# Another order of steps around the join behind attention and in the second experts' preparation

## The chip, the cores and the metric

The kernel runs on one core of a Trainium2 chip. The metric is the device time of one execution in microseconds. TensorE does matmuls, VectorE and ScalarE elementwise work and reductions, GpSimd (POOL) elementwise work and the indirect transfers; the SyncE queue (SP) issues the plain loads and stores.

## What is computed

Three layers, one behind the other, in float32: an attention with local and global keys, a mixture of experts with soft slots, and a mixture of experts in which each token takes its two best experts by noisy scores.

```python
def reference(**kwargs):
    attn_out = _attn_ref(**attn_kwargs)          # batch 2, 8 heads, 768 positions, head size 64
    x = np.ascontiguousarray(attn_out.transpose(0, 2, 1, 3)).reshape(B * S, H * D)   # 1536 x 512
    x = _moe_ref(x=x, **moe_kwargs)              # 32 slots in 8 experts, softmax over tokens and over slots
    return _moe2_ref(x=x, **moe2_kwargs)         # 8 experts, two per token

def _moe2_ref(x, w_gate, w_noise, noise, w1, w2):
    logits = x @ w_gate
    noise_scale = np.log1p(np.exp(x @ w_noise))
    noisy_logits = logits + noise_scale * noise
    top2 = np.argpartition(-noisy_logits, 2, axis=1)[:, :2]
    ...
            h = np.maximum(x[mask] @ w1[e], 0.0)
            out[mask] += top2_w[mask, k, None] * (h @ w2[e])
```

## The kernel before

**Attention** goes over 12 tiles of 128 tokens. While it runs, the soft slots' sums (maxima, exponentials, weighted tokens) are carried along by segments of tiles. **The join** (lines 541 to 612) adds the last tile: `psl` holds its logits in PSUM, `rn` the running negative maxima, `pm` gathers the maxima of the partition groups, `mneg` is their minimum. ScalarE copies the last tile's tokens from PSUM (`xl`, line 574), forms the factor of the old sums (`wun`, 581) and the new exponentials (`Et`, 582). TensorE adds up old sums (`joined`, 592) and the new tile (603) into `psi`, which VectorE copies to `siT` (608). `warm(k)` issues k matmuls whose result nobody uses. PE, DVE, ACT and POOL run in the order written here.

**The first experts** (`ffn_a`, `ffn_t`, `ffn_b`) start behind it: 8 experts, weights streamed in float32, the slots' 32 rows as stationary operand. Their result `op` in PSUM is copied in two halves into `os_` (770, 771), and eight matmuls (780) bring it into `soT`.

**The router** (954 to 991) forms the noisy scores: `ex` and `u_` are the exponential and one more than it, `ln` the logarithm (983), `t1` a correction of it (984 to 986). VectorE then takes the correction off, multiplies by the noise and adds the logits `pl` from PSUM (987 to 989) into `nl`, in which line 1005 looks for the best.

**The second experts** work in float16 pairs (high and low part). For each expert `e` a `Rank` object holds its steps, named by K0, K1, K2 for the first three: `w_abs(q)` (842) makes the maximum of a quarter of the second-layer weights on ScalarE, `w_scale_a` (850) joins the four on VectorE, `w_pow_a` (813) is a matmul that spreads it over the partitions, `w_pow_b` (821 to 828) makes the power of two by which the weights are scaled, `w_hi(q)` (871) writes a scaled quarter on ScalarE and `w_lo(q)` (874) the rest of it on VectorE; `inv` (922) keeps the inverse. `g_scale_a`, `g_hi`, `g_lo` and `g_put` do the same for the products of the first-layer weights with the slots' outputs (`Gst`). `pow_a` and `pow_b` do both powers of two in one.

The tokens are sorted into 24 slots of 128 rows, three per expert. `slot_h(j)` makes a slot's hidden values (1194), `slot_l` their low part (1203), and `slot_y(j)` is a generator of 24 matmuls (1282): for slots 0 and 1 each `next` issues two of them, and `go_on(ys, n)` calls `next` n times on each generator; for later slots each `next` issues eight. `add_out` adds the rows to the output by an indirect transfer (1300).

The order of slots 0 and 1 with the steps of K0, K1 and K2 is written out by hand from line 1487 on. For later slots the loop over `n` calls `do(n, place)` at the places "0", "l", "a", "m", "p", "e" and "b" between the blocks of eight matmuls, and `rank_steps` puts the steps of expert r at places counted in quarters of a slot from `BASE[r]`: `k(2, ...)` of expert 2 is place "m" of slot 3 and `k(3, ...)` its place "p".

Of the kernel before, what the change touches and what calls it, by code (L numbers as in the profile page):

```python
# [13 lines left out]
AF = mybir.ActivationFunctionType  # L14
ALU = mybir.AluOpType
# [46 lines left out]
def emit(tc, d, near=True, stop=None):  # L62
    nc = tc.nc
    es = ExitStack()
    with es:
# [122 lines left out]
        X = {}  # L188
# [361 lines left out]
        def warm(k):  # L550

            for _ in range(k):
                nc.tensor.matmul(pw, warmw[:, 0:128], warmw[:, 0:512], start=True, stop=True)
# [17 lines left out]
        if near:  # L571
            stX(NT - 1)
        xl = X["x", NT - 1]
        nc.scalar.activation(xl, X["pxx"].rearrange("p a q -> p (a q)"), AF.Copy)
        list(rest)
        mneg = cw.tile([128, 1], F32, name="mneg")
        nc.vector.tensor_reduce(mneg, pm, AX.X, ALU.min)
# [2 lines left out]
        wun = cw.tile([128, 1], F32, name="wun")  # L580
        nc.scalar.activation(wun, old, AF.Exp, bias=mneg, scale=-1.0)
        nc.scalar.activation(Et[P1], psl[P1], AF.Exp, bias=mneg[P1], accum_out=sg[P1])
        Wc = cw.tile([128, 32], F32, name="Wc")
        nc.vector.tensor_scalar(Wc, sel4[:, 0:32], wun, None, ALU.mult)
        sw = cw.tile([128, 1], F32, name="sw")
# [23 lines left out]
        nc.vector.tensor_scalar(rw, psum, 1e-9, None, ALU.add)  # L609
        nc.vector.reciprocal(rw, rw)  # L610
        nc.vector.tensor_copy(Ltok[:, NT - 1, :], pl_[:, 1, P1])
        warm(1)
        s_tail.close()
        s_ps.close()
        s_at.close()
# [31 lines left out]
        def pm_(shape, dt=F32):  # L647
            return ps_m.tile(shape, dt, name="m")
# [6 lines left out]
        def cut32(a, n):  # L655
            return more[:, a:a + n]

        wgn = cut32(0, 64).rearrange("p (c e) -> p c e", c=4)
        noise = cut32(64, 96).rearrange("p (t e) -> p t e", t=NT)
# [50 lines left out]
        def ring(i):  # L710
            return wst.tile([128, 2048], F32, name=f"w{i}")
# [10 lines left out]
        op = ps_y.tile([128, 512], F32, name="y")  # L722
# [45 lines left out]
        s_r.enter_context(tc.manual_schedule(engines=by_hand))  # L768
        os_ = wb.tile([128, 2048], F32, name=f"w{NWA + NW}")
        nc.scalar.activation(os_[:, 0:256], op[:, 0:256], AF.Copy)  # L770
        nc.scalar.activation(os_[:, 256:512], op[:, 256:512], AF.Copy)
        wy = ps_y.tile([128, 512], F32, name="y")

        def warm(k):
# [158 lines left out]
        K0, K1 = raw[0], raw[1]  # L933
# [22 lines left out]
        ttt = nc.vector.tensor_tensor  # L956
        gw = scratch([128, 4, 16], F32)
        ex, u_, ln, t1, rc, b_, nl = V("ex"), V("u_"), V("ln"), V("t1"), V("rc"), V("b_"), V("nl")
# [5 lines left out]
        pl = pm_([128, NT, 16])  # L964
# [19 lines left out]
        nc.vector.scalar_tensor_tensor(t1, u_, -1.0, ex, ALU.add, ALU.subtract)  # L984
        nc.vector.reciprocal(rc, u_)
        ttt(t1, t1, rc, ALU.mult)
        ttt(ln, ln, t1, ALU.subtract)
        ttt(ln, ln, noise, ALU.mult)
        ttt(nl, ln, pl[:, :, 0:8], ALU.add)
        K0.g_scale_a()  # L990
        nc.scalar.activation(gs0[:, 0:1], ex[:, 0, 0:1], AF.Exp)

# [193 lines left out]
        def slot_h(j, ct, hh=None, between=None):  # L1186
            e = j // OWN
            hh = wk3.tile([128, 2, 8, 128], F16, name="hh") if hh is None else hh
            phs = []
            for q in range(2):  # L1190
                ph = ps_h.tile([128, 4, 128], F32, name="h")
                for i in range(4):
                    f = 4 * q + i
                    nc.tensor.matmul(ph[:, i], Gst[:, e, 128 * f:128 * f + 128], ct, start=True, stop=True)  # L1194
                nc.scalar.activation(hh[:, 0, 4 * q:4 * q + 4], ph, AF.Relu)  # L1195
                phs.append(ph)
                if q == 0 and between:
                    between()
            return hh, phs
# [162 lines left out]
        def fetch(r, i):  # L1362

            t = xr(i) if i < 2 else ring(2 * ((r + 1) % 2) + i - 2)
            raw.setdefault(r, Rank(r, {})).u[i] = load_part(r, i, t)
# [3 lines left out]
        def at(j, place, f, *a):  # L1369
            steps.setdefault((j, place), []).append((f, a))  # L1370
# [5 lines left out]
        def rank_steps(r):  # L1376


            def k(place, nm, *a):
                j, q = divmod(BASE[r] + place, 4)  # L1380
                at(j, "0amp"[q], lambda: fetch(*a) if nm == "fetch" else getattr(raw[r], nm)(*a))

            first = r == 2
            if not first:
                k(-3, "g_mm")
            for i in range(2):
                if 2 < r < NE - 1:
                    k(-2, "fetch", r + 1, i)
            if not first:
                k(-2, "g_scale_a")  # L1390
                for q in range(4):
                    k((-4, -3, -1, 0)[q], "w_abs", q)
            if first:
                at(3, "l", K2.w_scale_a)
            else:
                k(0, "w_scale_a")
            k(2, "pow_a")
            k(2, "pow_b")
            k(3, "g_hi")
            k(4, "g_lo")  # L1400
            k(4, "w_hi", 0)
            k(4, "g_put", 0)
            k(5, "w_hi", 1)
            k(5, "g_put", 1)
            k(5, "w_lo", 0)
            k(6, "w_hi", 2)
            k(6, "w_lo", 1)
            if 2 < r < NE - 2:
                k(6, "fetch", r + 2, 2)
            k(8, "inv")  # L1410
            k(8, "w_hi", 3)
            k(9, "w_lo", 2)
            k(10, "w_lo", 3)
            if 2 < r < NE - 2:
                k(10, "fetch", r + 2, 3)
# [3 lines left out]
        for r in range(2, NE):  # L1419
            rank_steps(r)  # L1420
# [13 lines left out]
        def go_on(ys, n):  # L1434
            for _ in range(n):
                for y in ys:
                    next(y)
# [59 lines left out]
        for i in range(2):  # L1497
            K1.g_end(i, pst[i])
        h = slot_h(2, t)
        K1.w_pow_a()  # L1500
        K2.g_scale_a()
        go_on((y1,), 4)
        K1.w_pow_b()
        go_on((y0,), 2)
        list(y0)
        K1.w_hi(0)
        go_on((y1,), 4)
        list(y1)
        K1.w_hi(1)
        K0.inv()  # L1510
        K1.w_hi(1)
        K0.inv()
        h = slot_l(*h)
# [32 lines left out]
        with tc.If(over > 4):  # L1546
            t0, t1, t2, t3 = ring(0).bitcast(F16), ring(1), ring(2).bitcast(F16), ring(3).bitcast(F16)
# [205 lines left out]
```

## Time and profile before

| | us |
|---|---|
| median of 3 runs | 330.26 (330.18 to 330.68) |
| profiled execution, whole time | 330.27 |
| its span, first to last instruction | 328.2 |
| TensorE busy | 304.8 (93%) |
| ScalarE busy | 207.2 (63%) |
| VectorE busy | 200.1 (61%) |
| GpSimd busy | 132.4 (40%) |
| mean granted TensorE clock | 0.988 of full |

The busy shares are means over stages of different kinds, so the stages are read one by one below. In the rows, PE is TensorE, PEld its weight loads, DVE VectorE, ACT ScalarE; L and a number is a line of the kernel; times are microseconds from the span's start. What stands in brackets at a row's end is the idle time of the engine ahead of it and what ended that.

### The profile page before, as it was taken

The numbers are of one execution on the slowest core, as the hardware profiler recorded it, in microseconds if no ns is written. First come the engines' busy times: TensorE is split into PE (matmuls) and PEld (weight loads), VectorE is DVE, ScalarE is ACT, GpSimd is POOL, SyncE is SP. The second block draws the span as 40 slices with busy tenths as digits, with TensorE's granted clock in tenths as the row PEclk, the third lists the DMA queues.
The fourth block names the chain that finished last, engine by engine and source line by source line (L and its number), as shares of the span: only waits on it lengthen the run. The fifth ranks groups of instructions, "written<-read, shape, count | busy, mean of one in ns | idle before, by whom it ended". The sixth has DMA issues, their size and how long they took to land. (4 is left out here: it accounts for less than half of the span.)

```text
span 328.2 us, 7762 instructions
## 1 busy us (share of the span) xinstructions
PE 304.8 (93%) x2861; PEld 170.3 (52%) x2861; DVE 200.1 (61%) x723; ACT 207.2 (63%) x492; POOL 132.4 (40%) x165
## 2 busy tenths in 40 slices
PE   8699999999999999998989899999999999999990
PEld 3467776677775444344544444554454445544540
DVE  1965666656654100079787696978677595997210
ACT  2787777887632211089859795967778686785310
POOL 2364653554420010114450968561825445352131
PEclk9999999999997999999999999999999999999997
DMA  8999979847899999999899999489798943404342
GB/s 251 372 405 349 384 245 369 311 170 262 331 408 409 409 408 404 410 406 381 317 330 376 409 183 314 65 267 337 229 306 307 346 90 44 64 7 47 52 66 38
DMA packets 30571, 89.25 MB, mean 272 GB/s; under 512 B 2736, under 2 KB 6576, under 8 KB 30528
## 3 DMA queue, kind: packets, MB, share of 16 engines
q1 hardware_dynamic: 25840, 80.70, 65.1%
q0 software_dynamic: 4400, 7.48, 14.7%
q10 hardware_dynamic: 288, 0.52, 0.6%
q8 instruction: 24, 0.39, 0.5%
q14 instruction: 19, 0.16, 0.1%
HBM read 78.55 MB, written 10.14 MB: 270 GB/s over the span
## 5 line engine op out<-in xcount | busy, mean ns | idle before, releaser
L1282 PE MATMUL y<-w2hl,hh 128*128 128x512 f16 x552 | 125.0, 379 | 0.0
L1282 PEld LDWEIGHTS <-hh 128*128 128x128 f16 x552 | 52.2, 98 | 60.8 <-issue 3.5
L211 ACT ACTIVATE Tt<-Tt,nm 128x167 f32<-128x167 f32 x96 | 40.8, 428 | 20.7 <-DVE nm L204 20.6
L226 POOL TENSOR_TENSOR Pb<-Tt,r 128x668 f32<-128x668 f32 x24 | 31.6, 1318 | 47.8 <-DVE r L218 26.5
L1203 DVE SCALAR_TENSOR_TENSOR hh<-h,hh 128x512 f16<-128x512 f32 x46 | 29.5, 683 | 20.3 <-ACT hh L1195 20.2
L1300 POOL DMA_INDIRECT out_y<-ys,sidx x15 | 28.0, 1863 | 28.5 <-ACT ys L1294 14.4
L874 DVE SCALAR_TENSOR_TENSOR w2hl<-w,pm,w2hl 128x1024 f16<-128x1024 f32 x28 | 35.2, 1279 | 4.1 <-ACT w2hl L871 3.2
L1318 POOL DMA_INDIRECT cT<-ctab,gidx x25 | 29.5, 1179 | 12.0 <-issue 6.8
L204 DVE CUSTOM_DVE_ANT_0 Tt<-s,bias 128x167 f32<-128x167 f32 x96 | 26.0, 327 | 11.8 <-PE s L200 10.1
L1195 ACT ACTIVATE hh<-h 128x512 f16<-128x512 f32 x46 | 25.1, 595 | 12.1 <-PE h L1194 11.9
L871 ACT ACTIVATE w2hl<-w,pm 128x1024 f16<-128x1024 f32 x29 | 32.4, 1146 | 0.2 <-DVE pm L827 0.2
L842 ACT ACTIVATE w2hl<-w 128x1024 f16<-128x1024 f32 x28 | 29.5, 1056 | 0.0
L236 PE MATMUL pt<-c,Pb 128*128 128x128 f32 x176 | 26.5, 282 | 2.9 <-ACT PT L240 1.6
L240 ACT ACTIVATE PT<-pt 128x512 f32<-128x512 f32 (+1 forms) x48 | 26.0, 546 | 2.3 <-PE pt L236 2.3
L200 PE MATMUL s<-kx,qd 64*64 64x167 f32 x384 | 22.4, 313 | 4.1 <-DVE nm L204 3.0
L1300 POOL DMA_INDIRECT out_y<-c,sidx x7 | 12.5, 1789 | 32.0 <-DVE hh L1203 14.9
L236 PEld LDWEIGHTS pt<-c,Pb 128*128 128x128 f32 x176 | 18.6, 141 | 11.3 <-ACT PT L240 4.1
L259 PE MATMUL px<-PT,vt 128*64 128x128 f32 x352 | 22.3, 277 | 0.2
L200 PEld LDWEIGHTS s<-kx,qd 64*64 64x64 f32 x384 | 14.9, 132 | 11.0 <-PE pt L236 5.0
L259 PEld LDWEIGHTS px<-PT,vt 128*64 128x64 f32 x352 | 18.9, 137 | 3.0 <-issue 1.9
L211 ACT ACTIVATION_READ_ACCUMULATOR Tt<-Tt,nm 128x1 f32 x96 | 18.5, 193 | 0.0
L704 PE MATMUL h<-w,siT 128*32 128x256 f32 x256 | 16.4, 404 | 0.0
(314 smaller groups left out, 445.5 us busy)
## 6 DMA issues: line engine op xcount, KB each, us to landing
w<-in_w2b SPq DMA_DIRECT2D x14, 1024.0 KB, 7.4
x<-in_w1b SPq DMA_DIRECT2D x12, 1024.0 KB, 14.4
w<-in_w1a SPq DMA_DIRECT2D x16, 512.0 KB, 7.7
w<-in_w2a SPq DMA_DIRECT2D x16, 512.0 KB, 6.6
w<-in_w1a SPq DMA_DIRECT2D x8, 1024.0 KB, 8.6
w<-in_w2a SPq DMA_DIRECT2D x8, 1024.0 KB
vt<-in_va SPq DMA_DIRECT2D x6, 512.0 KB, 8.0
out_y<-w2hl SPq DMA_DIRECT2D x1, 3072.0 KB
```

What stands on the lines that cost most here:

```text
L200: nc.tensor.matmul(st[t][r:r + 64, n % 2, :], qd[T % NQ][g, p, 64 * t:64 * t + 64], kx[g, p, a:a + 167], start=True, stop=True, tile_posit ...
L211: nc.scalar.activation(Tt[:, k], Tt[:, k], AF.Exp, bias=nm[:, k:k + 1], scale=-1.0, accum_out=st[:, k:k + 1])
L226: nc.gpsimd.tensor_tensor(wide(Pn, 33, 264 + 64, 528, 167), Pu.rearrange("p (a t) c -> p a t c", t=2), rb(167), ALU.mult)
L236: nc.tensor.transpose(pt[:, ch, t], Pn[:, 2 * (n % 2) + t, 136 * ch:136 * ch + 128], ident)
L259: nc.tensor.matmul(px[64 * h:64 * h + 64, p, :], vv[:, c:c + 64], cols_, start=(ch == 0 or m == 0), stop=(ch == 1))
L842: nc.scalar.activation(w2hl[:, self.r, 1, 2 * q:2 * q + 2], self.quarter(q), AF.Abs, accum_out=self.wm[:, q:q + 1])
L871: nc.scalar.activation(w2hl[:, self.r, 0, 2 * q:2 * q + 2], self.quarter(q), AF.Copy, scale=self.sw)
L874: nc.vector.scalar_tensor_tensor(w2hl[:, self.r, 1, 2 * q:2 * q + 2], self.quarter(q), self.sw, w2hl[:, self.r, 0, 2 * q:2 * q + 2], ALU.m ...
L1203: nc.vector.scalar_tensor_tensor(hh[:, 1, 4 * q:4 * q + 4], phs[q], 0.0, hh[:, 0, 4 * q:4 * q + 4], ALU.max, ALU.subtract)
L1282: nc.tensor.matmul(py, hh[:, hx, f], w2hl[:, e, wx, f], start=(n == 0), stop=(n == 23))
L1300: o = nc.gpsimd.indirect_dma_start(out=out, out_offset=bass.IndirectOffsetOnAxis(ap=sidx[:, j:j + 1], axis=0), in_=ys, in_offset=None, com ...
L1318: nc.gpsimd.indirect_dma_start(out=cgf[:, place(n)], out_offset=None, in_=ctab, in_offset=bass.IndirectOffsetOnAxis(ap=gidx[:, n:n + 1], a ...
```

## The change

Seven small moves, with no new function:

- In the join, ScalarE's copy into `xl` stands behind the two exponentials instead of ahead of them, and one `warm(1)` at its end goes.
- The second half of the copy into `os_` goes from ScalarE to VectorE.
- The router's sum is formed as (logits - correction x noise) + logarithm x noise instead of (logarithm - correction) x noise + logits.
- `pow_a` and `pow_b` of expert 2 move from place "m" of slot 3 to its place "p", ahead of `g_hi`.
- `K1.w_pow_a` moves behind `K2.g_scale_a` and behind eight matmuls of slot 1.
- `K1.w_hi(1)` and `K0.inv()`, which stand there twice, are made once.

```diff
         xl = X["x", NT - 1]
-        nc.scalar.activation(xl, X["pxx"].rearrange("p a q -> p (a q)"), AF.Copy)
         list(rest)
...
         nc.scalar.activation(Et[P1], psl[P1], AF.Exp, bias=mneg[P1], accum_out=sg[P1])
+        nc.scalar.activation(xl, X["pxx"].rearrange("p a q -> p (a q)"), AF.Copy)
...
         nc.vector.tensor_copy(Ltok[:, NT - 1, :], pl_[:, 1, P1])
-        warm(1)
...
         nc.scalar.activation(os_[:, 0:256], op[:, 0:256], AF.Copy)
-        nc.scalar.activation(os_[:, 256:512], op[:, 256:512], AF.Copy)
+        nc.vector.tensor_copy(os_[:, 256:512], op[:, 256:512])
...
         ttt(t1, t1, rc, ALU.mult)
-        ttt(ln, ln, t1, ALU.subtract)
+        ttt(t1, t1, noise, ALU.mult)
+        ttt(t1, pl[:, :, 0:8], t1, ALU.subtract)
         ttt(ln, ln, noise, ALU.mult)
-        ttt(nl, ln, pl[:, :, 0:8], ALU.add)
+        ttt(nl, ln, t1, ALU.add)
...
-            k(2, "pow_a")
-            k(2, "pow_b")
+            k(2 + first, "pow_a")
+            k(2 + first, "pow_b")
             k(3, "g_hi")
...
         h = slot_h(2, t)
-        K1.w_pow_a()
         K2.g_scale_a()
         go_on((y1,), 4)
+        K1.w_pow_a()
         K1.w_pow_b()
         go_on((y0,), 2)
         list(y0)
         K1.w_hi(0)
         go_on((y1,), 4)
         list(y1)
-        K1.w_hi(1)
-        K0.inv()
         K1.w_hi(1)
         K0.inv()
```

## Rows read from the trace of the kernel before

**Rows 1.** Table of stretches: us; busy us per engine, instructions in brackets; clock, DMA share, GB/s.

```profile
180.00:200.00 20.00, 19.02 (x133) 9.47 (x132) 16.19 (x39) 16.70 (x31) 15.53 (x14) 1.00 0.98 312
200.00:220.00 20.00, 20.00 (x140) 10.20 (x138) 16.90 (x52) 15.72 (x27) 12.22 (x14) 1.00 0.73 183
```

**Rows 2.** Timeline of the join: start us, us, engine, line, operation, out and in.

```profile
98.50 0.27 DVE L578 COPY Lsb<-psl 32x128 f32<-32x128 f32 x1
98.63 0.60 ACT L574 ACTIVATE xs<-pt 128x512 f32<-128x512 f32 x1 [2.63 <-PE pt L276]
...
99.12 0.28 ACT L581 ACTIVATE wun<-rn,mneg 128x1 f32<-128x1 f32 x1
99.31 0.34 ACT L582 ACTIVATE Et<-psl,mneg 32x128 f32<-32x128 f32 x1
...
100.94 1.06 PE L603 MATMUL o<-Et,xs 128*128 128x32 f32 x8
...
102.37 0.61 PE L553 MATMUL pt<-c 128*128 128x512 f16 x1
...
102.50 0.17 DVE L611 COPY Ltok<-s 128x32 f32<-128x32 f32 x1
...
102.91 4.92 PE L704 MATMUL h<-w,siT 128*32 128x256 f32 x64
```

**Rows 3.** Stretches of half a microsecond, TensorE alone: busy us, granted clock, DMA share, GB/s.

```profile
102.00:102.50 0.50, 0.50 (x4) 0.59 1.05 418
...
105.50:106.00 0.50, 0.50 (x16) 0.99 1.06 426
```

**Rows 4.** Timeline, the copies of the slot outputs.

```profile
136.64 0.38 ACT L770 ACTIVATE w<-y 128x256 f32<-128x256 f32 x1 [5.63 <-PE y L750]
...
137.08 1.08 PE L780 MATMUL m<-c,w 128*128 128x32 f32 x8 [0.50 <-ACT w L770]
```

**Rows 5.** Timeline, the last slot's copy, split between VectorE and ScalarE.

```profile
319.76 0.48 DVE L1291 TENSOR_SCALAR ys<-y,gsc 128x256 f32<-128x256 f32 x1 [6.87 <-PE y L1282]
320.29 0.47 ACT L1292 ACTIVATE ys<-y,gsc 128x256 f32<-128x256 f32 x1 [5.01 <-DVE ys L1291]
```

**Rows 6.** Timeline, the router: first operation behind the logarithm, and the search.

```profile
142.35 0.26 DVE L987 TENSOR_TENSOR w2hl<-w2hl 128x96 f32<-128x96 f32 x1 [0.16 <-ACT w2hl L983]
...
143.29 0.92 DVE L1005 MAX8 w2hl<-w2hl 128x8 f32<-128x8 f32 x12
```

**Rows 7.** Timeline of TensorE at expert 1's power of two.

```profile
166.68 0.61 PE L1194 MATMUL h<-ct,Gst 128*128 128x128 f16 x8
...
168.92 0.23 PE L813 MATMUL m<-identb,wx 128*128 128x128 bf16 x1 [1.63 <-DVE wx L850]
...
168.98 1.89 PE L1282 MATMUL y<-w2hl,hh 128*128 128x512 f16 x8
...
170.71 1.03 PE L1282 MATMUL y<-w2hl 128*128 128x512 f16 x4
```

**Rows 8.** Timeline, ScalarE's scaled quarters of expert 1.

```profile
173.99 3.36 ACT L871 ACTIVATE w2hl<-w,pm 128x1024 f16<-128x1024 f32 x3
```

**Rows 9.** Loads issued in 141 to 142.5 us (last: landing), and the timeline's first use.

```profile
w<-in_w2b SPq DMA_DIRECT2D x2, 1024.0 KB, 8.0
...
158.83 1.06 ACT L842 ACTIVATE w2hl<-w 128x1024 f16<-128x1024 f32 x1
```

**Rows 10.** Timeline at expert 2's powers of two, and its scaled rows.

```profile
183.13 0.22 PE L813 MATMUL m<-identb,gm 128*128 128x128 bf16 x1
...
184.11 0.16 DVE L850 TENSOR_REDUCE wx<-wm 128x1 f32<-128x4 f32 x1 [1.98 <-ACT w2hl L842]
...
184.40 3.62 PE L1282 MATMUL y<-w2hl,hh 128*128 128x512 f16 x16
...
191.80 0.73 DVE L919 COPY Gst<-Gst 32x1024 f16<-32x1024 f16 x1
...
193.53 0.61 PE L1194 MATMUL h<-ct,Gst 128*128 128x128 f16 x8
```

## The prediction

> **What bounds the kernel now.** I read the table of stretches first [rows 1]. In 200 to 220 us TensorE is busy all the time at the full clock, and the three stretches after it, up to 280 us, read the same; in 180 to 200 it lacks 0.98 us. From about 184 us on the end is therefore TensorE's start plus a fixed row of matmuls: what lets that row start one microsecond earlier ends the kernel one microsecond earlier. Before that point the chain runs through several engines, so I went along the timeline and looked at the places that the diff touches: the join behind attention at 98 us, the copies at 137 us, the router's VectorE chain at 142 us, and the second experts' preparation at 166 to 194 us. The question in each is which wait ends last.
>
> The transfers are the other candidate: the DMA share is 0.98 in 180 to 200 us [rows 1]. But no compute instruction of the path waits for a load after 92 us. The second-layer weights of expert 1, issued from 141.3 on, land 8.0 us later, by about 150, and ScalarE first reads them at 158.83 [rows 9]: about 9 us in hand, more than all that I forecast.
>
> **The join: copy moved behind the exponentials.** The join's row of work is ScalarE's copy (98.63), its exponential of the old maxima (99.12), its exponential of the new logits (99.31), then VectorE and TensorE. The exponentials stand behind the copy only by ScalarE's order: the copy takes the slot from 98.63 to 99.12, 0.49 us [rows 2]. What the first exponential needs VectorE writes just ahead of its own copy at 98.50; the second reads the PSUM tile that this copy reads from 98.50 to 98.77, and in the new order it starts at about 98.82, just behind. So everything from here to the first expert's matmul moves by 0.49 us. The moved copy would end at about 99.8; its readers, the join's last eight matmuls (100.94 before), would start at 100.45, so other work covers it by 0.6 us. Were it later than that, only the amount beyond would count.
>
> **The join: one warm-up matmul removed.** It starts at 102.37 and takes 0.61 us, and the first expert's matmul starts at 102.91, although VectorE's last copy, for which it waits, ended at 102.67 [rows 2]. Handing over from VectorE costs about 0.05 us where a row shows it [rows 5], so the start could have been 102.72: 0.18 us lost. With both edits the experts start 0.67 us earlier, at about 102.23.
>
> **What the clock takes back.** The granted clock falls to its lower level, 1.2 GHz, at 102.1 us, behind a join in which TensorE has only small matmuls, and is at 2.4 GHz again from 105.5 (0.50 in all six half-microseconds between the two rows) [rows 3]. If that low stretch stays where it is, the 0.67 us of earlier start are worked at half speed: by 105.5 the kernel before has done (105.5 - 102.9)/2 = 1.30 us of full-speed work, the changed one (105.5 - 102.23)/2 = 1.63. The gain is 0.33 us; if the low stretch moves along with the work it is 0.67. I take 0.33, since nothing ahead of 98.6 moves, and keep both ends.
>
> **The split copy of the slot outputs.** The second half goes from ScalarE to VectorE. TensorE starts on the first half at 137.08, and its eight matmuls stand evenly (0.28 us each, 1.08 in all, so one per 0.114) [rows 4]: none of them waited for the second half, and the fifth, the first that needs it, is due at 137.54. A faster second half wins nothing. It could lose: at the end of the kernel one PSUM tile is split in the same way, and there ScalarE starts at 320.29, when VectorE's 0.48 us are over, after an idle wait for it [rows 5]. One behind the other, VectorE would end at 136.64 + 0.38 + 0.48 = 137.50 plus 0.05 or 0.1 of handing over. Price: 0 (side by side) to 0.1 us; I take 0, as 137.5 is still about when it is due.
> The Trainium skill (PSUM — Partial Sum Buffer, "PSUM bank collisions raise a hardware error") says that ScalarE and VectorE must not read the same partitions of one bank at once, so that software has to put them in sequence; the trace agrees, with 320.29 behind 319.76 + 0.48. By that rule this part of the sum is a loss of 0 to 0.1 us, by the opposite it is 0.
>
> **The router's chain.** Before, three VectorE operations follow the logarithm, and the first waited 0.16 us for ScalarE until 142.35; the search starts at 143.29, so they take 0.94, or 0.31 each [rows 6]. After, two operations run ahead without the logarithm and two follow: four from about 142.2. In a strict chain that is 4 x 0.31 = 1.25, ending at 143.44, a loss of 0.15; with the third overlapped, since it does not depend on the two ahead of it, the loss is about 0. I take 0.05 us. It is on the path: the search follows at once.
>
> **Expert 1's power of two, placed later.** TensorE ends the hidden matmuls that start at 166.68 (eight of them, some 0.05 us apart) by about 167.1 and then stands until 168.92 (1.63 us idle by the profile), because the little matmul next in its queue needs a maximum that VectorE gives only then. Behind it stand eight matmuls of slot 1, from 168.98 to 170.71, which need nothing of it [rows 7]. The change puts these eight ahead. They take 1.73 us, run from about 167.1 to 168.85, and the little matmul still starts at about 168.92. What followed at 170.71 then starts at 168.97: 1.74 us gained. VectorE's reading of the result is not delayed, and ScalarE's copy of slot 0 and the scaled quarters behind it move along.
>
> **Steps made twice removed.** One of ScalarE's three scalings that start at 173.99 and take 3.36 us is the second copy of the same step: about 1.1 us of ScalarE [rows 8], and a tiny VectorE operation. TensorE waits for neither directly. Their worth is that all later ScalarE work of this stretch, among it expert 2's absolute maxima, comes 1.1 us earlier on top of the 1.74.
>
> **Expert 2's power of two, one place later.** TensorE's next stall is of the same kind: one little matmul at 183.13, the other only behind VectorE's last maximum of expert 2 (184.11, it had waited 1.98 us for ScalarE), and slot 3's last eight matmuls not before 184.40 [rows 10]. The change puts both little matmuls behind those eight. With the 1.74 and 1.1 us above, the maximum is there at about 181.3, while the pair is due at about 183.1, so it does not stall again. Gained: 184.40 - 183.13 = 1.27 less the pair's own 0.12 (0.06 each, from 168.92 to 168.98 in [rows 7]) = 1.15 us. In exchange the chain behind the pair stands later in the order: the scaled rows of expert 2, copied last by VectorE from 191.80 to 192.53 and first used by TensorE at 193.53, 1.00 us in hand [rows 10]. TensorE moves by 1.74 + 1.15 = 2.89. If this chain moves by as much, nothing is lost; if only by the 1.74, it costs 2.89 - 1.74 - 1.00 = 0.15. I take 0. No transfer is moved past another; the loads issued behind these steps go out earlier with them.
>
> **The sum.** 0.33 - 0 - 0.05 + 1.74 + 1.15 = 3.17 us. The profiled execution took 330.27 us (span 328.2 and 2.07 around it) and the median is 330.26, so no scaling is needed: 330.27 - 3.17 = 327.1 us.
>
> **Rivals.**
> The clock stays up. The new join is denser, shorter by 0.67 us. If the clock then does not fall, the start gains its 0.67 and the 1.30 us lost at half clock besides: 1.97 in place of 0.33, giving 325.5 us. For it: the fall came only at the very end of the join [rows 3]. Against it: up to 102.1 the new order holds nearly the same matmuls. Chance 0.16. The Trainium skill (TensorE: Matmul & The Clock Gate, "The HAM clock gate") says that TensorE's activity sets its clock and that the moment of a change varies from run to run; the fall at 102.1 agrees with the first, no row here shows the second.
> The gain is partly given back at expert 2's first slot. If its scaled rows do not move at all, TensorE waits 2.89 - 1.00 = 1.89 us there (329.0); halfway between that and the 0.15 above it is 328.1 us. For it: VectorE is busy 16.2 of 20 us there [rows 1], and the pair stands 1.73 us later in TensorE's order. Against it: ScalarE's queue gets 1.1 us free. Chance 0.14.
> The transfers set the pace after all. If the weights of experts 3 and 4 had no slack, TensorE would wait for them in 180 to 200 us and end where it does now, 330.2 us. For it the DMA share of 0.98 [rows 1], against it the 9 us of [rows 9]. Chance 0.05.
> Slower: the clock stays down. Without the warm-up matmul the low stretch could be longer. At half clock each microsecond of dense work costs 0.5; to eat 3.17 us the clock would have to stay down 6.3 us beyond 105.5, to about 112 us, and from there on the kernel is slower: with 114 us it takes 331.4. Against it: the experts' matmuls follow without a gap, and they brought the clock back at 105.5 before [rows 2, 3]. Chance 0.04.
>
> **How the numbers follow.** The forecast has 0.61, with its own range 326.5 to 327.7 (the bounds 0.33 to 0.67 at the join, 0 to 0.25 lost at copy and router, 0.15 at expert 2). For 8 in 10 the range reaches to the free clock, 325.3, and into the partly lost gain, 328.4. A difference of 0.2%, 0.66 us, is about what a measurement of this kernel tells from none. Faster by more: the forecast, the free clock and the partial loss, 0.91; within: the transfers, 0.05; slower: 0.04.
>
> **What would show it.** In the new profile the first expert's matmul starts near 102.2; TensorE has no idle wait for a maximum near 167 to 169 and none near 181 to 183; slot 3's last eight matmuls start some 3 us earlier; the busy row of 200 to 280 us stays unbroken and ends earlier by the same. I am wrong if a wait of TensorE appears ahead of expert 2's first slot near 190 us, if a load is what an engine waits for, or if the low clock lasts beyond 106 us.

## The result and the profile after

The changed kernel takes 328.38 us (median of 11 runs, 327.45 to 329.87) beside 331.48 us for the kernel before, measured with it (11 runs, 329.4 to 334.39): a ratio of 0.9907 with a 95% interval of 0.9879 to 0.9935. The forecast of 327.1 us was 0.9904 of the 330.26 us known then. The profiled execution after took 327.62 us, with a span of 325.7; before it was 330.27 and 328.2. Both kernels scatter by 2 to 5 us from one execution to the next; a section below shows one cause. Executions more than 1.5% above the fastest of their kernel are left out of all ratios, so a ratio need not be that of two medians.

The rows after are shown in the order of the rows before; line numbers are those of the kernel that ran, so they differ by one here and there. First the table of stretches (us; busy us of PE, PEld, DVE, ACT, POOL; clock, DMA share, GB/s), which answers to [rows 1]:

```profile
180.00:200.00 20.00, 20.00 (x141) 10.03 (x139) 14.28 (x35) 16.06 (x30) 13.40 (x15) 1.00 1.01 332
200.00:220.00 20.00, 20.00 (x141) 10.29 (x140) 16.69 (x52) 14.57 (x25) 13.62 (x15) 1.00 0.76 179
```

The 0.98 us that TensorE lacked in 180 to 200 us are filled. The join, against [rows 2]:

```profile
98.38 0.27 DVE L577 COPY Lsb<-psl 32x128 f32<-32x128 f32 x1
98.49 0.29 ACT L580 ACTIVATE wun<-rn,mneg 128x1 f32<-128x1 f32 x1 [2.62 <-DVE mneg L576]
98.76 0.36 ACT L581 ACTIVATE Et<-psl,mneg 32x128 f32<-32x128 f32 x1
...
99.12 0.57 ACT L582 ACTIVATE xs<-pt 128x512 f32<-128x512 f32 x1
...
100.32 1.06 PE L603 MATMUL o<-Et,xs 128*128 128x32 f32 x8
...
101.88 0.17 DVE L611 COPY Ltok<-s 128x32 f32<-128x32 f32 x1
...
102.11 1.08 PE L703 MATMUL h<-w,siT 128*32 128x256 f32 x8 [0.36 <-DVE Ltok L611]
```

Counted from VectorE's copy into Lsb, the first exponential comes 0.51 us sooner (0.11 us behind it, before 0.62), the join's last eight matmuls 0.50 sooner (1.94, before 2.44), and the first expert's matmul 0.68 sooner (3.73, before 4.41). The moved copy ends at 99.69, 0.63 us ahead of its readers at 100.32. The first expert's matmul now starts 0.06 us behind the end of the copy it waits for.

The copies of the slot outputs and the router, against [rows 4] and [rows 6]:

```profile
136.09 0.38 ACT L769 ACTIVATE w<-y 128x256 f32<-128x256 f32 x1 [5.63 <-PE y L749]
136.51 0.42 DVE L770 COPY w<-y 128x256 f32<-128x256 f32 x1 [3.76 <-ACT w L769]
136.53 1.09 PE L779 MATMUL m<-c,w 128*128 128x32 f32 x8 [0.50 <-ACT w L769]
...
141.26 0.26 DVE L985 TENSOR_TENSOR w2hl<-w2hl 128x96 f32<-128x96 f32 x1
...
142.66 0.92 DVE L1005 MAX8 w2hl<-w2hl 128x8 f32<-128x8 f32 x12
```

VectorE starts behind ScalarE's copy (136.09 + 0.38 = 136.47), so the halves go one after the other, as at the kernel's end [rows 5], and TensorE's eight matmuls take 1.09 us in place of 1.08.

ScalarE's scaled quarters of expert 1, two in place of the three of [rows 8]:

```profile
172.40 2.18 ACT L870 ACTIVATE w2hl<-w,pm 128x1024 f16<-128x1024 f32 x2
```

TensorE at expert 1's power of two, and then at expert 2's, against [rows 7] and [rows 10]:

```profile
166.80 0.61 PE L1194 MATMUL h<-ct,Gst 128*128 128x128 f16 x8 [0.60 <-ACT ct L1101]
167.24 1.89 PE L1282 MATMUL y<-w2hl,hh 128*128 128x512 f16 x8
168.97 0.22 PE L812 MATMUL m<-identb,wx 128*128 128x128 bf16 x1
169.03 1.03 PE L1282 MATMUL y<-w2hl 128*128 128x512 f16 x4
...
173.85 0.33 PE L1194 MATMUL h<-ct,Gst 128*128 128x128 f16 x3 [0.29 <-DVE ct L1103]
...
180.03 3.62 PE L1282 MATMUL y<-w2hl,hh 128*128 128x512 f16 x16
183.49 0.22 PE L812 MATMUL m<-identb,gm 128*128 128x128 bf16 x1
183.54 0.22 PE L812 MATMUL m<-identb,wx 128*128 128x128 bf16 x1
183.60 1.89 PE L1282 MATMUL y<-w2hl,hh 128*128 128x512 f16 x8
185.33 0.61 PE L1194 MATMUL h<-ct,Gst 128*128 128x128 f16 x8
```

Both waits for a maximum are gone: the eight matmuls of slot 1 stand where TensorE stood still, and the pair of expert 2 runs through behind sixteen matmuls. Two new waits, 0.60 and 0.29 us, are taken up below. From slot 2's hidden matmuls (L1194) to the last slot's copy the kernel before takes 319.76 - 166.68 = 153.08 us [rows 5, 7], the changed one 317.25 - 166.80 = 150.45. This stretch is the measure used below, since it shuts out most of what happens ahead of it; where the part ahead ends some 2 us early (e4, e5, e7 below) even this stretch changes by some 0.3 us.

### The profile page after: what moved, and what is told of

It reads as the page before. It is cut to its first block, busy times and chain, and to the rows that moved or that the text cites. A ratio compares the mean times of both kernels' runs of the same rounds, so it can differ in the third digit from the quotient of the medians.

```text
span 325.7 us, 7762 instructions
## 1 busy us (share of the span) xinstructions
PE 304.1 (93%) x2860; PEld 170.2 (52%) x2860; DVE 199.6 (61%) x724; ACT 206.0 (63%) x490; POOL 131.8 (40%) x165
## 5 line engine op out<-in xcount | busy, mean ns | idle before, releaser
L1300 POOL DMA_INDIRECT out_y<-ys,sidx x15 | 27.0, 1797 | 27.4 <-ACT ys L1294 14.2
L1318 POOL DMA_INDIRECT cT<-ctab,gidx x25 | 28.5, 1141 | 12.0 <-DVE w2hl L1203 5.5
L870 ACT ACTIVATE w2hl<-w,pm 128x1024 f16<-128x1024 f32 x28 | 31.2, 1147 | 0.2 <-DVE pm L826 0.2
L1300 POOL DMA_INDIRECT out_y<-c,sidx x7 | 13.9, 1982 | 33.9 <-DVE hh L1203 14.9
L211 ACT ACTIVATION_READ_ACCUMULATOR Tt<-Tt,nm 128x1 f32 x96 | 18.5, 193 | 0.0
```

The source lines that it names most:

```text
L211: nc.scalar.activation(Tt[:, k], Tt[:, k], AF.Exp, bias=nm[:, k:k + 1], scale=-1.0, accum_out=st[:, k:k + 1])
L870: nc.scalar.activation(w2hl[:, self.r, 0, 2 * q:2 * q + 2], self.quarter(q), AF.Copy, scale=self.sw)
L1300: o = nc.gpsimd.indirect_dma_start(out=out, out_offset=bass.IndirectOffsetOnAxis(ap=sidx[:, j:j + 1], axis=0), in_=ys, in_offset=None, com ...
L1318: nc.gpsimd.indirect_dma_start(out=cgf[:, place(n)], out_offset=None, in_=ctab, in_offset=bass.IndirectOffsetOnAxis(ap=gidx[:, n:n + 1], a ...
```

## The experiments

"Tail" is that stretch, "join" goes from VectorE's maximum of the last tile's logits (L565) to the first expert's matmul (before 6.04 us, after 5.36). Ratios are times over those of the kernel before, measured with each run, with 95% intervals.

**Each of the three edits of the second experts alone.** On the kernel before, the power of two of expert 1 placed later:

```diff
-        K1.w_pow_a()
         K2.g_scale_a()
         go_on((y1,), 4)
+        K1.w_pow_a()
         K1.w_pow_b()
```

> The kernel before with one move alone: expert 1's little power-of-two matmul behind the eight matmuls of slot 1. My theory (TensorE's two stalls are the bulk): the idle 1.63 us ahead of that matmul goes, everything behind is 1.74 us earlier, the stall at expert 2's powers stays (about 1.0 to 1.3 us, since ScalarE's queue is still as long); time 1.7 us less. Rival (the gain is at the join and in ScalarE's load, the stall is refilled by the next wait): 0 to 0.4 us less.

Ratio 0.9946 (0.9927 to 0.9966); tail 151.37 us, 1.71 less. TensorE in the timeline:

```profile
169.73 0.23 PE L813 MATMUL m<-identb,wx 128*128 128x128 bf16 x1
...
183.42 0.23 PE L813 MATMUL m<-identb,wx 128*128 128x128 bf16 x1 [0.98 <-DVE wx L850]
```

The first stall goes and the second stays, whole. Stall 1 is worth what the prediction gave it (1.74).

On the kernel before, expert 2's pair one place later:

```diff
-            k(2, "pow_a")
-            k(2, "pow_b")
+            k(2 + first, "pow_a")
+            k(2 + first, "pow_b")
```

> The kernel before with expert 2's two little matmuls one place later, alone. My theory: slot 3's last eight matmuls run at once, the wait for VectorE's maximum at 183 to 184 us disappears behind them, 1.15 us less, and the first stall (1.63 us at 167 to 169) stays. Rival (the wait returns at the first use of expert 2's scaled rows, which had 1.0 us in hand): a wait of TensorE ahead of that use near 193 us and less than half of the gain, 0 to 0.5 us.

Ratio 0.9959 (0.9931 to 0.9988); tail 152.16, 0.92 less. The pair no longer waits, and up to slot 5's hidden matmuls 1.15 us are won (20.02 us behind slot 2's, before 21.17); but then expert 2's first slot waits for its scaled rows:

```profile
192.96 0.74 DVE L919 COPY Gst<-Gst 32x1024 f16<-32x1024 f16 x1
193.75 0.45 PEld L1194 LDWEIGHTS <-Gst 128*128 128x128 f16 x8 [0.54 <-DVE Gst L919]
```

That is the prediction's second rival, a part given back at expert 2's first slot: 1.15 - 0.92 = 0.23 us, when this edit stands alone. The scaled rows end 25.86 us behind slot 2's hidden matmuls, before 25.85, so they did not move, while TensorE gained 1.15 against the 1.00 that the prediction found in hand.

On the kernel before, the steps made twice made once:

```diff
         K1.w_hi(1)
         K0.inv()
-        K1.w_hi(1)
-        K0.inv()
```

> The kernel before with the steps that were made twice made once, alone. My theory, worked out further: ScalarE is 1.1 us earlier from 175 us on, expert 2's last maximum comes at about 183.1 instead of 184.11, and so most of TensorE's second stall goes without any move of the little matmuls: about 1.0 us less, and the first stall stays. Rival (the removed ScalarE step hides under TensorE's work and is worth nothing alone): 0.

Ratio 0.9967 (0.9939 to 0.9994); tail 151.95, 1.13 less. Expert 2's powers of two, and ScalarE's last maximum ahead of them:

```profile
182.18 1.05 ACT L842 ACTIVATE w2hl<-w2hl 128x1024 f16<-128x1024 f32 x1
...
183.36 0.16 DVE L850 TENSOR_REDUCE wx<-wm 128x1 f32<-128x4 f32 x1 [1.98 <-ACT w2hl L842]
183.56 0.22 PE L813 MATMUL m<-identb,gm 128*128 128x128 bf16 x1
183.61 0.22 PE L813 MATMUL m<-identb,wx 128*128 128x128 bf16 x1
```

The pair is at its old place and has no wait: the maximum of 183.36 is there when the pair is due. So without the twice-made step, 1.1 us of ScalarE in front of the maxima, the second stall does not arise. The prediction had booked that step as worth nothing by itself.

**The changed kernel with expert 2's pair back at place "m".**

```diff
-            k(2 + first, "pow_a")
-            k(2 + first, "pow_b")
+            k(2, "pow_a")
+            k(2, "pow_b")
```

> The changed kernel with expert 2's two little matmuls back at the earlier place. If the once-made steps and the first move already bring expert 2's maximum in time (181.50 in the changed kernel's trace against 181.76, when slot 3's second eight matmuls end), this costs nothing: the time of the changed kernel, 2.6 to 3.2 us under the kernel before. Rival (the move of the pair is what removes the second stall, as the sum of the prediction books it): a stall near 181.8 us and about 1.1 us more than the changed kernel.

Ratio 0.989 (0.9852 to 0.9928), beside 0.9907 with the move; tail 150.13 us, 2.95 less than before. The timeline shows the pair at 179.83 and 179.89 behind a maximum of 179.63, with no wait. This execution is one of those with the part ahead early, so its tail alone proves little. But from slot 3's hidden matmuls to the last copy it takes 143.39 us (315.31 - 171.92), the changed kernel 143.40 in both its profiles (317.25 - 173.85 and, in e11 below, 317.83 - 174.43), the kernel before 144.54. And in e11, where nothing ahead is early, the maximum (182.14) comes 0.20 us before place "m" is due (180.61 + 1.73 = 182.34), as it does here (179.63 and 179.83). With the step made once, the move to place "p" is worth nothing that these runs show. The other two edits alone sum to 1.71 + 1.13 = 2.84, the whole of the 2.88 measured below but for 0.04.

**The join's two edits alone.** The copy behind the exponentials, with the warm-up matmul kept (e5), and the warm-up matmul taken out, with the copy in its old place (e6):

```diff
-        nc.scalar.activation(xl, X["pxx"].rearrange("p a q -> p (a q)"), AF.Copy)
...
         nc.scalar.activation(Et[P1], psl[P1], AF.Exp, bias=mneg[P1], accum_out=sg[P1])
+        nc.scalar.activation(xl, X["pxx"].rearrange("p a q -> p (a q)"), AF.Copy)
```

> The kernel before with the join's copy behind the two exponentials, alone. My theory: the exponential of the old maxima starts about 0.5 us earlier against VectorE's copy just ahead of it, the first expert's matmul too (0.49 us), and the time is 0.25 to 0.5 us less, by where the low clock falls. Rival (the copy becomes late and the join's last eight matmuls wait for it): those matmuls wait for ScalarE and nothing is gained.

```diff
         nc.vector.tensor_copy(Ltok[:, NT - 1, :], pl_[:, 1, P1])
-        warm(1)
```

> The kernel before without the one warm-up matmul at the join's end, alone. My theory: the first expert's matmul starts 0.1 to 0.2 us earlier behind VectorE's last copy, the time is 0 to 0.2 us less. Rival (the matmul holds the clock): the low-clock stretch at 100 to 108 us, seen as 3.4 us in two profiles, 6.8 in two and absent in one so far, becomes longer or more frequent, and the median is 0.5 to 1.5 us more.

The order alone: ratio 0.9949 (0.9917 to 0.9981), join 5.36 us. Its profile has the clock up at the join; the old join with the clock up takes 5.86 us (102.66 - 96.80 in e10 below), so the order is worth 0.50. By the ratio it is 0.6 to 2.8 us, more than the 0.25 to 0.5 expected; whether the new order also makes the low clock rarer is taken up below. The warm-up matmul alone: 0.9994 (0.9952 to 1.0036), nothing that an interval of 1.4 us either way can tell. In e5's profile the clock is up throughout the join, and there the warm-up matmul costs nothing:

```profile
101.30 0.39 PE L553 MATMUL pt<-c 128*128 128x512 f16 x1
101.50 0.17 DVE L611 COPY Ltok<-s 128x32 f32<-128x32 f32 x1
101.73 0.58 PEld L704 LDWEIGHTS h<-w,siT 128*32 128x32 f32 x14 [0.34 <-DVE Ltok L611]
```

At the upper clock it takes 0.39 us and ends at 101.69, as the copy that the first expert waits for anyway is handed over (101.67 and 0.06). The 0.18 us that the prediction gave it exist only where the low clock stretches it to 0.61 [rows 2]. e6 agrees: there the clock is low, and without the matmul the first expert starts 0.23 us behind the start of VectorE's last copy (102.39, 102.62); in e1, as low and with the matmul, it is 0.40 (102.39, 102.79).

e5's tail is 152.74 us, 0.34 less than before, although nothing behind the join was edited: TensorE waits 0.54 us ahead of slot 2 for a gather (see below), so the maxima come earlier against it: its two stalls are 0.92 and 0.78 us (before 1.63 and 0.98), and a new one of 0.55 stands at slot 3.

**More work in the join, to hold the clock.** The changed kernel with three more warm-up matmuls where TensorE waits in the join:

```diff
         nc.vector.tensor_copy(Lsb[P1], psl[P1])
-        warm(2)
+        warm(3)
...
         nc.tensor.transpose(pl_[:, 1, P1], Lsb[P1], ident[P1, P1])
+        warm(2)
```

> The changed kernel with three more warm-up matmuls in TensorE's idle slots of the join (one more at 98.9, two more at 101.6 us), which delay nothing if they run at the full clock. If TensorE's activity in the join decides on the clock, low stretches at 100 to 108 us become rarer or shorter and the median falls by 0.5 to 1 us against the changed kernel; if so little does not decide, it is the same within 0.3 us.

Ratio 0.9867 (0.9819 to 0.9915). No low clock in its join, but there was none either in three kernels without these matmuls (table below), so the run does not tell whether they did it. The three added matmuls were not free: the join took 5.47 us in place of 5.36. Its time is not separable from the changed kernel's.

**Slot 3's rows transposed earlier**, so that the wait of 0.29 us at 173.85 has more cover; the changed kernel with

```diff
+        t = slot_t(3)
         K1.w_lo(0)
         rows()
-        t = slot_t(3)
```

> The changed kernel with VectorE's copy of slot 3's tokens placed ahead of the first low quarter of expert 1, behind which it came 0.15 to 0.29 us too late for TensorE at 174 us. My theory: that wait goes and the time is 0.15 to 0.3 us less than the changed kernel's. Rival (the wait moves to expert 1's low parts, which are now 0.2 us later): the same time.

Ratio 0.9865 (0.9816 to 0.9913); slot 3's hidden matmuls follow at 172.71 without a wait, tail 150.08 us, 0.13 less than that of the unedited kernel in e11. The interval overlaps the changed kernel's, so no better version is shown.

**The two small edits between, alone.** On the kernel before, the second half of the slot outputs' copy on VectorE (e9), and the router's new sum (e10):

```diff
-        nc.scalar.activation(os_[:, 256:512], op[:, 256:512], AF.Copy)
+        nc.vector.tensor_copy(os_[:, 256:512], op[:, 256:512])
```

> The kernel before, with only the second half of the copy into os_ given to VectorE. Question: in the changed kernel the router's exponential stood 2.11 us behind the slot outputs' matmuls, in the kernels built on the kernel before 2.24 to 2.25; which of two edits brought the 0.13 us. Theory A (the split; ScalarE is free earlier): 2.11 us here, and 0 to 0.1 us lost at the copies. Theory B (the router's sum): 2.24 us here. No difference that can be measured in the time.

```diff
-        ttt(ln, ln, t1, ALU.subtract)
+        ttt(t1, t1, noise, ALU.mult)
+        ttt(t1, pl[:, :, 0:8], t1, ALU.subtract)
         ttt(ln, ln, noise, ALU.mult)
-        ttt(nl, ln, pl[:, :, 0:8], ALU.add)
+        ttt(nl, ln, t1, ALU.add)
```

> The kernel before, with only the router's sum in the new order. Theory A: the exponential 2.24 us behind the slot outputs' matmuls, as before. Theory B: 2.11 us. From the exponential to the search for the best: 2.85 us before, 2.89 in the changed kernel; here 2.89 if the new order costs its 0.04 us by itself. No difference that can be measured in the time.

From the end of the slot outputs' matmuls (VectorE's copy into soT) to the router's exponential: 2.12 us with the split alone, 2.25 with the sum alone, 2.24 before. Theory A holds: the split brings 0.12 to 0.13 us. It lies in two hand-overs from TensorE: with the split VectorE (L962) starts 0.07 us behind the matmuls that it waits for and ScalarE's exponential 0.09, without it 0.13 and 0.16. Why they are shorter is not shown. From the copy into soT to the search it is 4.94 us with the split, 5.14 with the sum, 5.09 before and 5.00 after: the new sum costs 0.05, the split wins 0.15.

**Both kernels once more, unedited.**

> The changed kernel once more, nothing edited. Question: were the late hand-overs from TensorE at 166.5 and 170.2 us in its profile (1.55 and 1.0 us behind the end of the matmul) the program's or that execution's. If the program's: they stand there again, and slot 2's hidden matmuls to the last copy take 150.45 us. If the execution's: they are gone and it takes 150.1 to 150.2. The low clock at the join (101.8 to 105.2 us) may stand elsewhere; if place and length belong to the program, it stands there again.

> The kernel before once more, nothing edited. Question: does the low clock at the join belong to the program (then again 102.1 to 105.5 us, 3.4 us long) or to the execution (then elsewhere, longer, or absent, as it was in kernels that differ from this one only far behind the join). From slot 2's hidden matmuls to the last copy: 153.08 us as before, within 0.1.

The tail of the kernel before repeats (153.09 us). The changed one's is 150.21 in this execution, without the two waits of its first profile: those were that execution's. (The 1.55 us of the expectation is ScalarE's idle time; it started 1.1 us behind the end of the matmul.) Instead the clock was low from 100.5 to 107.4 us, which the prediction had named, beyond 106, as a sign of being wrong, and once more from 155.1 to 158.6. The two unedited pairs give a tail gain of 2.63 and 153.09 - 150.21 = 2.88 us.

## What makes one kernel's times scatter

Half-microsecond stretches of TensorE (busy, granted clock, DMA share, GB/s) of the first profile after, which answer to [rows 3]:

```profile
101.50:102.00 0.50, 0.25 (x2) 0.80 1.06 426
102.00:102.50 0.50, 0.39 (x4) 0.50 1.01 401
...
105.00:105.50 0.50, 0.50 (x12) 0.79 1.01 401
```

The low stretch is from 101.8 to 105.2 us here. Read in the same way for the other executions, with the time from the first expert's matmul to the first copy of the slot outputs beside it:

| execution | low clock at the join, us | experts, us |
|---|---|---|
| before, and once more | 102.1 to 105.5; 102.5 to 105.9 | 33.73; 33.88 |
| after, and once more | 101.8 to 105.2; 100.5 to 107.4 | 33.98; 35.27 |
| e1 (join as before) | 100.4 to 107.2 | 34.65 |
| e2 (join as before) | 101.1 to 107.9 | 34.94 |
| e3, e9 (join as before) | 102.8 to 106.1; 102.4 to 105.8 | 33.95; 33.85 |
| e6 (no warm-up matmul) | 100.5 to 107.3 | 34.75 |
| e8 (join as after) | 101.8 to 105.2 | 34.01 |
| e10 (join as before) | none | 32.48 |
| e4 (join as after), e5, e7 | none | 32.48 |

Low is 0.50, the lower level of 1.2 GHz. One and the same join shows 0, 3.4 or 6.8 us of it, with and without the warm-up matmul, and it costs 0, 1.25 to 1.55 or 2.2 to 2.8 us. With the exponentials first it is absent in 3 of 6 profiles, with the old order in 1 of 8; so few do not show whether the new order makes it rarer, and e5's ratio leaves that open. Where the join has none, it stands earlier: within 14.2 to 17.8 us in e4, e5 and e7 and from 15.0 to 18.5 in e10, where the other ten profiles run at the full clock. There it delays nothing that shows: the maximum at the join's start comes at 96.29 to 96.80 us in these four, at 96.03 to 97.19 in the others. Two rows of e4 and then one of the kernel before:

```profile
15.00:16.00 1.00, 1.00 (x5) 0.50 1.05 372
16.00:17.00 1.00, 1.00 (x3) 0.50 1.07 393
```

```profile
15.00:16.00 1.00, 1.00 (x18) 1.00 1.05 373
```

These differences are as large as the whole change; the 5 us between the kernel before's fastest and slowest execution are more than they explain. e10, which by its edit should gain nothing, took 328.76 us in an execution with the clock up at the join (the kernel before, measured with it: 331.31); a single time decides nothing here.

A free clock at the join is not all gain. In e4 the table of gates and tokens is stored from 152.49 us on, 2.45 us earlier than before (154.94), but lands 6.5 us later, in place of 3.7, and the gather for slot 2 starts at 159.88 as before (159.91). Before, by the profile, the gather waited last for VectorE's row numbers (L1466); in e5, as early as e4, the profile names the store, and in e4 TensorE then waits for the gather. A row of e5, then one of e4:

```profile
159.67 1.19 POOL L1318 DMA_INDIRECT cT<-ctab,gidx  x1 [7.19 <-DMA ctab<-c]
```

```profile
164.25 0.23 PE L1098 MATMUL m<-k,cT 128*128 128x128 f16 x1 [0.59 <-DMA cT<-ctab,gidx]
```

The stretches around the store, of e4 and then of the kernel before:

```profile
152.50:158.50 6.00, 5.56 (x72) 1.00 1.03 408
```

```profile
152.50:158.50 6.00, 4.74 (x38) 1.00 0.90 331
```

With the front early, the transfers run without a gap and set the pace; before, they had 10% to spare. In e4 the slot outputs' copy is 2.37 us earlier than before (134.27), and slot 2's transposition (L1098) only 1.51 (164.25, before 165.76): 0.86 us are swallowed. In e10, whose copy is 1.50 us earlier, nothing is yet (30.07 us to slot 2's hidden matmuls, before 30.04).

## Why the prediction was right, and where not

**The join.** Forecast 0.67 us earlier, measured 0.68, by the two parts as worked out: 0.50 from the order, 0.18 from the warm-up matmul, in profiles with the low clock in nearly the same place. With the clock up on both sides it is 0.50 (e10 against e5), since the warm-up matmul then costs nothing: the 0.18 was a price of the low clock. Up to the slot outputs' copy the gain was forecast as 0.33 (0.67 at most) and is (136.64 - 96.87) - (136.09 - 96.75) = 0.43. That the low stretch stays where it is was only nearly right: it came 0.3 us earlier with the work. As a forecast of the median the term is weak, since the low stretch differs from run to run by more than the term. The rival "the clock stays up" came in e4, e5 and e7, and also in e10 with the join as before: it belongs to the execution at least as much as to the edit.
The Trainium skill (TensorE: Matmul & The Clock Gate, "The HAM clock gate"), cited in the prediction, has the moment of a change vary from run to run; the table above agrees: after the old order the fall comes at 100.4 to 102.8 us, or not at all.

**The split copy and the router.** Forecast -0 and -0.05, measured +0.15 and -0.05, together a gain of 0.09 us (5.09 against 5.00). The rows that the price was read from [rows 5, 6] gave each its right size (the third operation did overlap: it starts at 142.09, ahead of the end of the second, 141.91 + 0.26); the gain came at the exponential, a place that I had not looked at.
The Trainium skill (PSUM — Partial Sum Buffer, "PSUM bank collisions raise a hardware error") wants the two readers in sequence; 136.51 behind 136.09 + 0.38 agrees. What the prediction drew from it, a loss of 0 to 0.1 us, was 0.01 at the matmuls.

**Expert 1's power of two.** Forecast 1.74, alone 1.71. Right, and for the stated reason.

**Steps made once, and expert 2's power of two.** Forecast nothing and 1.15, together 1.15; alone 1.13 and 0.92, together with the first edit 2.88 - 1.71 = 1.17. The size is right and the step it was booked to is wrong. The two edits each remove the same stall: making the step once brings the maximum 1.1 us earlier, which suffices by itself, and placing the pair later lets it wait in cover. What failed is the booking: "TensorE waits for neither directly" is true, but it waited for the step through ScalarE's queue and VectorE's last maximum, and [rows 10] showed it, since VectorE's maximum had waited 1.98 us for ScalarE. The prediction's own numbers said so: with the first edit the pair is due at its old place at 183.13 - 1.74 = 181.39, and the maximum was put at 181.3, so next to nothing of the stall is left for the move. I had the two edits in one sum and did not ask what each would do without the other.

**Given back at expert 2's first slot.** The rival did not come in the whole change: VectorE's last copy of the scaled rows ends at 190.34 and the matmuls start at 191.01, 0.67 us in hand. It came, with 0.23 us, where the move was made alone (e2): the scaled rows stayed where they were, which is the case that the rival described.

**The transfers.** As a rival it was put in 180 to 200 us, and there it did not come. It came at 153 to 160 us, in two of the four executions with the clock up at the join (TensorE waits 0.59 us in e4 and 0.54 in e5). The 9 us in hand of [rows 9] were those of one load, and not of the store that the gather waits for. The prediction's "no compute instruction of the path waits for a load" looked for loads and passed over a store that is read back.

**The sum.** 3.17 us forecast; 3.10 by the medians, with an interval of 2.2 to 4.0 us on 331.48 (0.9935 and 0.9879). The agreement of 3.17 and 3.10 is luck to the extent that the interval is 0.9 us either way. The time itself, 328.38, lies outside the forecast's own range of 326.5 to 327.7 and at the edge of the wider one (328.4), because the kernel before stands at 331.48 and not at the 330.26 of its first three runs. The two profiles differ by 330.27 - 327.62 = 2.65: the maximum at the join's start comes 0.12 earlier, then 0.43 are won up to the slot outputs' copy, 0.67 lost up to slot 2's hidden matmuls (30.04 us before, 30.71 after), 2.63 won in the tail, and 0.15 around the span; 0.12 + 0.43 - 0.67 + 2.63 + 0.15 = 2.66. The loss of 0.67 is the late hand-over below. Without it slot 2 comes 29.95 us behind the copy (e8). With the low stretch of 3.4 us on both sides and no other disturbance the edits are then worth 0.43 + 0.09 + 2.88 = 3.40 us by the profiles; the forecast lay within 0.3 of that. With the clock up on both sides the first term is 0.50 (38.34 us from the maximum to the copy in e10, 37.84 in e4).

## What to carry to other kernels

Two edits that remove the same stall do not add up: ask of each what is late if it stands alone, and follow an engine's queue back behind the wait before a removed step is called worthless. A stall in which an in-order engine waits for a small operation, with ready work queued behind it, is priced well by that ready work. And where one kernel's own executions differ by as much as the change, compare stretches between two of its own events and not whole times, and see to it that both sides reach the first event alike.

## What the runs showed of the hardware

**The clock** is above: 0, 3.4 or 6.8 us low at the same join, and, in the second execution after, 3.4 us at 155.1 to 158.6, where none of the other 13 profiles has it.

**Late hand-overs from TensorE.** In the first profile after, ScalarE starts on a matmul's result 1.1 us late: the matmul runs from 165.12 to 165.34 and ScalarE, idle, starts at 166.47. In the second, the same operation starts 0.25 us behind the matmul's start:

```profile
166.47 0.28 ACT L1101 ACTIVATE ct<-m 128x128 f16<-128x128 f16 x1 [1.55 <-PE m L1098]
```

```profile
166.70 0.22 PE L1098 MATMUL m<-k,cT 128*128 128x128 f16 x1
...
166.95 0.28 ACT L1101 ACTIVATE ct<-m 128x128 f16<-128x128 f16 x1 [0.48 <-PE m L1098]
```

VectorE's start on expert 1's maximum at 170.16, for a matmul that ended at 169.19, is of the same kind, and so are two in e7 (VectorE at 169.70 for a matmul that ended at 166.81, ScalarE at 169.76 for one that ended at 167.67), where TensorE then waits 0.95 and 1.10 us. They appear in 2 of 14 profiles, all in 165 to 171 us. What delays them was not found, and it stays open.
